# Loading x and wk in alternating halves, computing the first segment's K by token halves in four chunks, and casting its Q on ScalarE

## The chip, the cores and the metric

The kernel runs on 1 core of one Trainium2 chip. The metric is the device time of one execution in microseconds (us). Engines are called by the names of the profile: PE is TensorE's matrix multiply and PEld its weight load, DVE is VectorE, ACT is ScalarE, POOL is GpSimd, and SP is SyncE, which here only issues DMAs.

## What is computed

Two branches on the same 2048 x 512 input x (bf16) are mixed by a gate per token. Branch A is attention in four segments of 512 tokens, 32 heads of 16, with a memory carried from segment to segment; branch B is a gated GELU feed-forward with 1792 hidden units. Cut to what matters:

```python
q, k, v = x @ wq, x @ wk, x @ wv            # as (H=32, N=4 segments, L=512, Dh=16)
for s in range(N):
    logits = einsum('hqd,hkd->hqk', q[s], k[s]) * Dh**-0.5 + causal_mask
    a_dot = softmax(logits) @ v[s]
    a_mem = (phi(q[s]) @ M) / (phi(q[s]) @ z + 1e-6)
    outs.append(g * a_mem + (1 - g) * a_dot)
    M = M + phi(k[s]).T @ v[s];  z = z + sum(phi(k[s]))
a = concat(outs) @ wo
b = (gelu(x @ w_gate) * (x @ w_up)) @ w_down
out = sigmoid(x @ gate_w) * a + (1 - sigmoid(x @ gate_w)) * b
```

## The kernel before

**Layout.** Matmuls want the contracted dimension on the partitions, so x is held transposed: `xS[s]` is 128 x 4 x 512 (feature inside a block, 4 blocks `fc`, token). K, Q, gate and up projections of a segment are made in pieces of 128 output columns: four matmuls, one for each `fc`, of 128 x 128 weights against 128 x 512 tokens, summed in one bank of PSUM (2 KB a partition). A "chunk" c of K or Q is 128 columns, that is 8 heads; there are 4 chunks (`NC8`) a segment. Four banks are handed out in turn by the pool `pgen` (tag `gen`); the other four banks are one tile, `lg`, of the pool `plg`, which takes the logits of one visit.

**Start.** `load_inputs` (L136) issues all first loads on SP's queue in program order: x's first segment in two halves of 256 tokens into `x0` (L139, where a partition gets two neighbouring rows, so 2 KB in one run), then wk in two halves of 256 columns (L134, runs of 512 bytes), wq in one piece (runs of 1 KB), the gate weights, wv, beta and w_gate. PE first runs matmuls on constants (`warm_up`, L163). Then `transpose_x0` (L177) turns `x0` into `xS[0]`: for each half 8 transposes of 128 x 128 on PE into two banks, one bank copied out by DVE (L189) and one by ACT (L191); the copy also puts the tokens back in order, since a partition held two neighbouring ones. All 16 transposes come before any of K.

**K, Q, V and gate of segment 0.** `u_k` (L372) makes one chunk of K: 4 matmuls (L376), a cast to bf16 into `ktb` by `cast` (L306), and two masked copies of it into `KTm` (L386), a ring of `NK` = 3 chunks; the masks of the first three chunks run on DVE, the others on POOL. At the start chunks 0, 1, 2 of K are made, then the 4 chunks of Q (`u_q`, L286). `cast` puts an eviction on ACT when the planner's clock of ACT says that it is free within a limit, else on DVE; the limit is 0 until the main loop, so all casts of the start are DVE's (L313). Then `load_rest` (L151) issues the remaining loads: a memset on DVE of two elements of `xS[1]` (L152) holds back the transposing load of the second segment (L131), behind which w_up, the third segment, w_down and wo stand in SP's queue. V, a small piece `zT`, and the 14 gate pieces of segment 0 follow, the latter evicted by ACT with GELU.

**Main loop.** 72 visits, each of which makes a tile of logits (`group_qk`, L632: up to 8 matmuls into `lg`, one exponential on ACT, L643, causal masks on POOL, L647). Between visits a planner written in Python fills PE with pieces of other work from streams (K, Q, V, gate, up, down, out, memory), each with a due time (`want`) and a condition (`when`); it keeps its own clocks of PE, DVE and ACT, and the order of every engine's instructions is what it emits. K's fourth chunk of segment 0 is the first piece of stream K: it may start at visit 5 (`clock[0] >= last(i - NK)`), when the ring has room. Its 4 matmuls, its cast and its two masks on POOL lie in this filler; `phi` of chunks 2 and 3 of `ktb` stands behind it. A flag computed on the device chooses a general path that does not run with these inputs.

Of the kernel before, what the change touches and what calls it, by code (L numbers as in the profile page):

```python
# [11 lines left out]
ALU = mybir.AluOpType  # L12

P = 128
# [5 lines left out]
FC = D // P  # L20
NC8 = H // 8
# [3 lines left out]
NK = 3  # L25
NX = 3
NB = 8
# [4 lines left out]
BF = dt.bfloat16  # L32
F32 = dt.float32
# [3 lines left out]
MM512 = 0.216  # L37
# [16 lines left out]
def kernel(  # L54
# [15 lines left out]
    nc = tc.nc  # L70
# [4 lines left out]
    x2 = A_x[0]  # L75
# [5 lines left out]
    plg = ctx.enter_context(tc.tile_pool(name="plg", bufs=1, space=bass.MemoryType.PSUM))  # L81
    pgen = ctx.enter_context(tc.tile_pool(name="pgen", bufs=4, space=bass.MemoryType.PSUM))

    def const(shape, dtype, name):
        return cpool.tile(shape, dtype, name=name, tag=name)

    xS = [const([P, FC, L], BF, f"x{i}") for i in range(NX)]
    wq = const([P, FC, D], BF, "wq")
    wk = const([P, FC, D], BF, "wk")
# [5 lines left out]
    ident = const([P, P], BF, "ident")  # L95
    bm = const([P, 8, 17], BF, "bm")
    eo = const([P, 2], F32, "eo")
# [7 lines left out]
    ktb = const([P, NC8, L], BF, "ktb")  # L105
# [4 lines left out]
    KTm = const([P, NK, NB, 2, 64], BF, "KTm")  # L110
# [14 lines left out]
    def gen(name):  # L125
        return pgen.tile([P, 512], F32, name=name, tag="gen")
# [3 lines left out]
    def x_seg(s):  # L130
        nc.sync.dma_start_transpose(xS[s % NX][:, :, :], x2[s * L:(s + 1) * L, :])  # L131

    def cols(dst, src):
        nc.sync.dma_start(dst[:, :, :], src.rearrange("(fc p) n -> p fc n", p=P))  # L134

    def load_inputs():  # L136
        half = L // 2
        for i in range(2):
            nc.sync.dma_start(x0[:, 2 * i:2 * i + 2, :],  # L139
                              x2[half * i:half * (i + 1), :].rearrange("(p k) d -> p k d", p=P))  # L140
        for i in range(2):
            n = slice(D // 2 * i, D // 2 * (i + 1))
            cols(wk[:, :, n], A_wk[:, n])
        cols(wq, A_wq)
        nc.sync.dma_start(gw4, gate_w.rearrange("(fc p) -> fc p", p=P))
        cols(wv[:, :, 0:D], A_wv)
        nc.sync.dma_start(beta[:, :], A_beta.rearrange("(o n) -> o n", o=1).to_broadcast((P, H)))
        for n in (slice(0, 4 * P), slice(4 * P, DFF)):
            cols(wga[:, :, n], B_w_gate[:, n])

    def load_rest():  # L151
        nc.vector.memset(xS[1][:, 0, 0:2], 0.0)  # L152
        x_seg(1)
        cols(wup, B_w_up)
        x_seg(2)
        cols(wdn, B_w_down)
        cols(wo, A_wo)


    x0 = G[1][:, 0:KT, :]  # L160
    gw4 = G[1][0:FC, KT, 0:P]

    def warm_up():  # L163
        T = gen("warm")
        for i in range(5):
            nc.tensor.matmul(T[:, :], lhsT=nc.const_aps.tensor(1.0, [P, P], BF),
                             rhs=nc.const_aps.tensor(1.0, [P, 512], BF), start=True, stop=True)

        U = gen("warm")
        for i in range(16):  # L170
            j, r = i // 2 % 4, i % 2
            nc.tensor.matmul((T, U)[r][32 * j:32 * j + 32, 0:256],
                             lhsT=nc.const_aps.tensor(1.0, [64, 32], BF, 64 * r),
                             rhs=nc.const_aps.tensor(1.0, [64, 256], BF, 64 * r),
                             start=True, stop=True, tile_position=(64 * r, 32 * j))

    def transpose_x0():  # L177
        for half in range(2):
            for f0 in range(0, FC, 2):
                T = pgen.tile([P, 1024], BF, name="x0T", tag="gen")  # L180
                for i in range(4):
                    fc, k = f0 + i // 2, i % 2
                    nc.tensor.transpose(T[:, i * P:(i + 1) * P],
                                        x0[:, 2 * half + k, fc * P:(fc + 1) * P], ident[:, :])
                dst = xS[0][:, f0:f0 + 2, half * 256:half * 256 + 256].rearrange(
                    "q f (p k) -> q f k p", k=2)
                src = T[:, 0:512].rearrange("q (f k p) -> q f k p", f=2, k=2)
                if f0 == 0:
                    nc.vector.tensor_copy(dst, src)  # L189
                else:  # L190
                    nc.scalar.copy(dst, src)  # L191

    def transpose_gw():
        T = pgen.tile([P, 1024], BF, name="gwT", tag="gen")
        nc.tensor.transpose(T[:, 0:FC], gw4, ident[0:FC, 0:FC])
        nc.vector.tensor_copy(wv[:, :, D], T[:, 0:FC])
# [89 lines left out]
    def u_q(s, c):  # L286
        def f():
            T = gen("qT")
            for fc in range(FC):
                nc.tensor.matmul(T[:, :], lhsT=wq[:, fc, c * P:(c + 1) * P],  # L290
                                 rhs=xS[s % NX][:, fc, :],
                                 start=(fc == 0), stop=(fc == FC - 1))
                if fc < FC - 1:
                    yield MM512
            cast(QT[:, c, :], T[:, :])
            return MM512
        return 4 * MM512, EVAC, f


    limit = [0.0]  # L300
    spared = [0.0]

    def near(end):
        return t_act[0] - 1.0 <= end and max(t_act[0], end) + CAST_T <= limit[0]

    def cast(out, src, scale=1.0):  # L306
        end = t_pe[0] + MM512
        if near(end):
            nc.scalar.activation(out, src, AF.Copy, scale=scale)
            t_act[0] = max(t_act[0], end) + CAST_T  # L310
            spared[0] = EVAC
        elif isinstance(scale, float):
            nc.vector.tensor_copy(out, src)  # L313
        else:
            nc.vector.tensor_scalar_mul(out, src, scale)
# [7 lines left out]
    general_now = [False]  # L323
# [43 lines left out]
    def u_phk(s, c):  # L367
        def f():
            phi(ktb[:, c:c + 2, :], ktb[:, c:c + 2, :], ("k", s, c), 1)
        return 0.0, 0.0, f  # L370

    def u_k(s, c):  # L372
        def f():
            T = gen("kT")
            for fc in range(FC):
                nc.tensor.matmul(T[:, :], lhsT=wk[:, fc, c * P:(c + 1) * P],  # L376
                                 rhs=xS[s % NX][:, fc, :],
                                 start=(fc == 0), stop=(fc == FC - 1))
                if fc < FC - 1:
                    yield MM512  # L380
            cast(ktb[:, c, :], T[:, :])
            if general_now[0]:
                return MM512
            for p in range(2):
                eng = nc.vector if s == 0 and c < NK else nc.gpsimd
                eng.tensor_scalar(out=KTm[:, (NC8 * s + c) % NK, :, p, :],  # L386
                                  in0=ktb[:, c, :].rearrange("q (b k) -> q b k", b=NB),
                                  scalar1=eo[:, p:p + 1], scalar2=None, op0=ALU.mult)
            return MM512
        return 4 * MM512, EVAC, f  # L390

    def turn(dst, src):
        T = pgen.tile([P, 1024], BF, name="tT", tag="gen")
# [294 lines left out]
    load_inputs()  # L688
    make_identity(nc, ident[:, :])
    warm_up()  # L690
    transpose_x0()
    setup_consts()


# [7 lines left out]
    def unit(u, want, key=None, when=None):  # L702
        return u + (key, when, want)
# [78 lines left out]
    def run(u):  # L782
        if u[0] == 0.0:
            u[2]()
        else:
            for _ in u[2]():
                pass

    for c in range(NK):
        run(u_k(0, c))  # L790
    for c in range(NC8):
        run(u_q(0, c))
    load_rest()
    transpose_gw()
    for kt in range(KT):
# [25 lines left out]
    def first(i):  # L821
        return 9 * (i // 2) + (1 if i % 2 == 0 else 5)

    def last(i):
        return 9 * (i // 2) + (5 if i % 2 == 0 else 9)

    us = [unit(u_phk(0, 0), 0)]
    for i in range(NK, NSEG * NC8):
        s, c = i // NC8, i % NC8
        us.append(unit(u_k(s, c), first(i) - 12, ("k", s),  # L830
                       lambda i=i, s=s, c=c: clock[0] >= last(i - NK) and
                       (s == 0 or count(("pk", s - 1)) > c)))
        if c % 2 == 1 and s < NSEG - 1:
            us.append(unit(u_phk(s, c - 1), 0, None,
                           lambda s=s: s == 0 or count(("pk", s - 1)) == NC8))
    streams.append(Stream("K", us))
    us = []
    for i in range(NC8, NSEG * NC8):
        s, c = i // NC8, i % NC8
# [5 lines left out]
    us = []  # L845
# [7 lines left out]
    us = []  # L853
# [16 lines left out]
    us = []  # L870
    for s in range(NSEG - 1):
# [9 lines left out]
    us = [unit(u_absmax_x(2, (18, 20, 22, 25)), 17, None, lambda: clock[0] >= 17),  # L881
           unit(u_absmax_x(3, (52, 55, 56, 60)), 51, None, lambda: clock[0] >= 51),
           unit(u_bound(), 61, None, lambda: clock[0] >= 61)]
    streams.append(Stream("Z", us))

    us = []
# [6 lines left out]
    us = []  # L893
# [5 lines left out]
    us = []  # L899
# [6 lines left out]
    us = []  # L906
# [73 lines left out]
    for pieces in visits:  # L980
        clock[0] += 1
        for i, b, off in pieces:
            s, c = i // NC8, i % NC8
# [4 lines left out]
        s = pieces[0][0] // NC8  # L988
        t = group_qk(pieces)
# [8 lines left out]
        if lumps and lumps[0][0] == clock[0]:  # L998
            i = lumps.pop(0)[1]
# [156 lines left out]
    for reg in flag:  # L1156
        i = 0 if reg.engine == mybir.EngineType.Pool else 1
# [32 lines left out]
```

## Time and profile before

| what | value |
|---|---|
| time, median of 3 runs (lowest, highest) | 269.92 us (269.92, 272.15) |
| time of the profiled execution | 269.92 us |
| its span, first to last instruction | 268.2 us |
| granted TensorE clock, mean | 0.999 |
| K's matmuls in all (L376), 64 of 128x512 | 16.8 us |
| Q's matmuls in all (L290), 64 | 16.6 us |
| logit masks on POOL (L647), 256 | 113.9 us |
| exponentials on ACT (L643), 72 | 135.1 us |
| masks of K on POOL (L386), 26 | 40.6 us, 1571 ns each |
| DMA, share of 16 engines | 23.4% for the program's own queue, 16.14 MB |

Times inside the profile are in us from the start of the span. In a timeline a row is: start, duration, engine, line, operation, output<-inputs, shape, count; what stands in brackets is the idle time of that engine ahead of it and what ended it. In the chain of waits a row is start, duration and what the end of the program was waiting for in that stretch. Matmuls overlap: a 128x512 matmul has a record of 380 ns, but twelve of them follow each other in 2.6 us, 0.216 us each.

### The profile page before, as it was taken

The page shows a single profiled execution, that of the slowest core. Times are in us where ns is not written, and L with a number is a line of the kernel's source. Part 1 is how long each engine was busy: PE and PEld are TensorE (multiplying, and loading weights), DVE is VectorE, ACT ScalarE, POOL GpSimd, SP SyncE. Part 2 cuts the span into 40 slices and gives each one's busy share as a digit, 9 for nine tenths or more (in the row PEclk, how much of TensorE's full clock was granted, in tenths as well). Part 3 has the DMA queues.
Part 4 walks back from the last instruction along what each step waited for, and adds up shares of the span by engine and source line. Part 5 has one row for each costly group of instructions (what it writes and reads, how often), then busy time and mean ns, then how long its engine had stood idle before and what let it go on. Part 6 is the DMA issues. An engine that isn't in the chain of part 4 may idle for free.

```text
span 268.2 us, 6580 instructions
## 1 busy us (share of the span) xinstructions
PE 262.7 (98%) x2713; PEld 118.0 (44%) x2713; DVE 204.0 (76%) x391; ACT 209.0 (78%) x163; POOL 156.9 (58%) x298
## 2 busy tenths in 40 slices
PE   7999999999999999999999999999999999999994
PEld 3454434344454444544444444434454544344441
DVE  2999575968778787697985979686889479698364
ACT  3236889999997998889999988889888987657510
POOL 4000158897905979987921998596785079655500
PEclk9999999999999999999999999999999999999999
DMA  6999911200070000301032001100000200003102
GB/s 213 304 197 329 341 36 39 42 4 0 20 145 2 0 22 22 78 4 42 0 61 62 4 21 42 42 20 22 20 24 21 66 2 20 2 20 42 40 22 83
DMA packets 30281, 16.59 MB, mean 62 GB/s; under 512 B 20008, under 2 KB 28968, under 8 KB 30248
## 3 DMA queue, kind: packets, MB, share of 16 engines
q1 hardware_dynamic: 30248, 16.14, 23.4%
q8 instruction: 22, 0.36, 0.6%
q14 instruction: 11, 0.09, 0.1%
HBM read 8.14 MB, written 2.10 MB: 38 GB/s over the span
## 4 chain that ended last, share of the span: by engine, by line
PE 87%; POOL 5%; issue 4%; DMA 2%; ACT 1%; SPq 0%; DVE 0%; ACTq 0%; DVEq 0%; POOLq 0%
PE gT L473 19%; PE uT L494 17%; PE dT L510 14%; PE lg L638 8%; PE od L663 6%; PE aT L527 5%; PE qT L290 5%; PE kT L376 5%; PE vT L414 4%; POOL pT L647 3%; POOL KTm L386 2%; DMA wk<-in_A_wk_dram 2%; PE MT L548 1%; PE mn L617 1%; ACT pT L643 1%
## 5 line engine op out<-in xcount | busy, mean ns | idle before, releaser
L647 POOL TENSOR_SCALAR_AFFINE_SELECT pT<-pT 64x256 bf16<-64x256 bf16 x256 | 113.9, 445 | 94.3 <-ACT pT L643 81.5
L643 ACT ACTIVATE pT<-lg 128x2048 bf16<-128x2048 f32 x72 | 135.1, 1876 | 24.9 <-PE lg L638 21.6
L494 PE MATMUL uT<-x,wup 128*128 128x512 bf16 x224 | 60.4, 380 | 0.0
L473 PE MATMUL gT<-x,wga 128*128 128x512 bf16 x224 | 57.0, 380 | 0.0
L510 PE MATMUL dT<-wdn,G 128*128 128x512 bf16 x224 | 52.9, 380 | 0.0
L500 DVE TENSOR_TENSOR G<-uT,G 128x512 bf16<-128x512 f32 x56 | 38.1, 684 | 6.4 <-PE uT L494 6.2
L386 POOL TENSOR_SCALAR KTm<-ktb,eo 128x512 bf16<-128x512 bf16 x26 | 40.6, 1571 | 1.3
L670 DVE STREAM_TRANSPOSE oq<-od 128x512 f32<-128x512 f32 x32 | 21.0, 695 | 19.3 <-PE od L663 19.3
L510 PEld LDWEIGHTS <-G 128*128 128x128 bf16 x224 | 20.8, 98 | 25.0 <-issue 2.1
L473 PEld LDWEIGHTS <-wga 128*128 128x128 bf16 x224 | 20.4, 98 | 23.9 <-issue 2.2
L494 PEld LDWEIGHTS <-wup 128*128 128x128 bf16 x224 | 19.8, 97 | 24.0 <-issue 5.4
L638 PE MATMUL lg<-QT,KTm 32*128 32x192 bf16 (+7 forms) x512 | 28.6, 287 | 0.0
L313 DVE CAST G<-gT 128x512 bf16<-128x512 f32 x24 | 16.5, 688 | 9.7 <-PE gT L473 9.5
L638 PEld LDWEIGHTS <-KTm 32*128 32x128 bf16 x512 | 8.3, 92 | 28.3 <-issue 28.0
L663 PE MATMUL od<-pT,V 64*32 64x128 bf16 (+7 forms) x512 | 19.4, 284 | 0.2 <-POOL pT L647 0.2
L663 PE MATMUL od<-pT,Vs 64*32 64x128 bf16 (+7 forms) x512 | 19.4, 284 | 0.0
L488 ACT ACTIVATE G<-G 128x3584 bf16<-128x3584 bf16 x6 | 18.8, 3182 | 0.0
L676 DVE SCALAR_TENSOR_TENSOR o<-oq,ogs,rden 128x256 bf16<-128x256 f32 x32 | 17.0, 532 | 1.1
L376 PE MATMUL kT<-x,wk 128*128 128x512 bf16 x64 | 16.8, 380 | 0.7 <-DMA wk<-in_A_wk_dram 0.7
L290 PE MATMUL qT<-x,wq 128*128 128x512 bf16 x64 | 16.6, 379 | 0.0
L532 DVE SCALAR_TENSOR_TENSOR tB<-aT,gct,tB 128x512 bf16<-128x512 f32 x16 | 11.9, 746 | 6.0 <-PE aT L527 5.7
L527 PE MATMUL aT<-wo,oT 128*128 128x512 bf16 x64 | 16.5, 380 | 0.0
(96 smaller groups left out, 276.0 us busy)
## 6 DMA issues: line engine op xcount, KB each, us to landing
out_dram<-tB SPq DMA_DIRECT2D x16, 128.0 KB, 1.7
wup<-in_B_w_up_dram SPq DMA_DIRECT2D x1, 1792.0 KB, 8.7
wdn<-in_B_w_down_dram SPq DMA_DIRECT2D x1, 1792.0 KB
wga<-in_B_w_gate_dram SPq DMA_DIRECT2D x1, 1280.0 KB, 10.5
Vs<-V SPq DMA_DIRECT2D x8, 144.0 KB, 2.6
G<-in_A_x_dram SPq DMA_DIRECT2D x2, 256.0 KB, 2.8
wk<-in_A_wk_dram SPq DMA_DIRECT2D x2, 256.0 KB, 4.5
wq<-in_A_wq_dram SPq DMA_DIRECT2D x1, 512.0 KB, 5.8
```

What stands on the lines that cost most here:

```text
L290: nc.tensor.matmul(T[:, :], lhsT=wq[:, fc, c * P:(c + 1) * P], rhs=xS[s % NX][:, fc, :], start=(fc == 0), stop=(fc == FC - 1))
L376: nc.tensor.matmul(T[:, :], lhsT=wk[:, fc, c * P:(c + 1) * P], rhs=xS[s % NX][:, fc, :], start=(fc == 0), stop=(fc == FC - 1))
L386: eng.tensor_scalar(out=KTm[:, (NC8 * s + c) % NK, :, p, :], in0=ktb[:, c, :].rearrange("q (b k) -> q b k", b=NB), scalar1=eo[:, p:p + 1], ...
L473: nc.tensor.matmul(T[:, :], lhsT=wga[:, fc, hs * P:(hs + 1) * P], rhs=xS[s % NX][:, fc, :], start=(fc == 0), stop=(fc == FC - 1))
L494: nc.tensor.matmul(T[:, :], lhsT=wup[:, fc, hs * P:(hs + 1) * P], rhs=xS[s % NX][:, fc, :], start=(fc == 0), stop=(fc == FC - 1))
L500: nc.vector.tensor_tensor(out=g, in0=T[:, :], in1=g, op=ALU.mult)
L510: nc.tensor.matmul(T[:, :], lhsT=G[s % NG][:, hs, qt * P:(qt + 1) * P], rhs=wdn[:, hs, :], start=(hs == 0), stop=(hs == HS - 1))
L527: nc.tensor.matmul(T[:, :], lhsT=oT[:, fc, qt * P:(qt + 1) * P], rhs=wo[:, fc, :], start=(fc == 0), stop=(fc == FC - 1))
L638: nc.tensor.matmul(lg[:, j, off:off + n], lhsT=KTm[rows, i % NK, b].rearrange("r p k -> r (p k)"), rhs=QT[rows, i % NC8, 64 * b:L], start= ...
L643: nc.scalar.activation(pT[:, :, :], lg[:, :, :], AF.Exp, scale=DH ** -0.5)
L647: nc.gpsimd.affine_select(out=v, in_=v, pattern=[[0, 4], [1, 64]], compare_op=ALU.is_ge, fill=0.0, base=0, channel_multiplier=-1)
L663: nc.tensor.matmul(od[p][32 * j:32 * j + 32, 64 * b:L], lhsT=w[:, 18 * h:18 * h + 32], rhs=t[rows, j, off:off + n], start=(b == 0), stop=( ...
```

## The change

The loads go out as x half, wk half, x half, wk half; x's rows are taken so that partition p holds row 128 k + p (runs of 1 KB in place of 2 KB), and the copies after the transposes no longer reorder. A new function `first_k` makes all four chunks of segment 0's K, each in two halves of 256 tokens (8 matmuls of 256 columns a chunk): chunks 0 and 1 in banks of the ring, 2 and 3 in two banks of the logits' tile. Its order on PE is: transposes of half 0; chunks 0 and 1 of half 0; transposes of half 1; chunks 2 and 3 of half 0; chunks 0 and 1 of half 1; chunks 2 and 3 of half 1. DVE casts chunks 0 and 2, ACT 1 and 3. Q's four casts go to ACT by a flag. The planner's unit for the fourth chunk now holds only its two masks on POOL, and its due time and condition stay. `setup_consts` now comes ahead of the transposes in the program, so DVE's two small sums of `eo` stand ahead of its copies.

```diff
         for i in range(2):
             nc.sync.dma_start(x0[:, 2 * i:2 * i + 2, :],
-                              x2[half * i:half * (i + 1), :].rearrange("(p k) d -> p k d", p=P))
-        for i in range(2):
+                              x2[half * i:half * (i + 1), :].rearrange("(k p) d -> p k d", p=P))
             n = slice(D // 2 * i, D // 2 * (i + 1))
             cols(wk[:, :, n], A_wk[:, n])
...
-    def transpose_x0():
-        for half in range(2):
-            for f0 in range(0, FC, 2):
...
-                dst = xS[0][:, f0:f0 + 2, half * 256:half * 256 + 256].rearrange(
-                    "q f (p k) -> q f k p", k=2)
-                src = T[:, 0:512].rearrange("q (f k p) -> q f k p", f=2, k=2)
...
+    def transpose_x0(half):
+        for f0 in range(0, FC, 2):
...
+            dst = xS[0][:, f0:f0 + 2, half * 256:half * 256 + 256]
+            src = T[:, 0:512].rearrange("q (f t) -> q f t", f=2)
...
     def cast(out, src, scale=1.0):
         end = t_pe[0] + MM512
-        if near(end):
+        if on_act[0]:
+            nc.scalar.copy(out, src)
+        elif near(end):
...
+    def u_km(s, c):
+        def f():
+            k_masked(s, c)
+        return 0.0, 0.0, f
+
+    def first_k():
+        lg = plg.tile([P, 4, 512], F32, name="lg", tag="lg")
+        Ts = {2: lg[:, 0, :], 3: lg[:, 1, :]}
+
+        def part(c, half):
+            t = slice(256 * half, 256 * half + 256)
+            for fc in range(FC):
+                nc.tensor.matmul(Ts[c][:, t], lhsT=wk[:, fc, c * P:(c + 1) * P], rhs=xS[0][:, fc, t],
+                                 start=(fc == 0), stop=(fc == FC - 1))
+
+        def evict(c):
+            if c % 2 == 0:
+                nc.vector.tensor_copy(ktb[:, c, :], Ts[c][:, :])
+            else:
+                nc.scalar.copy(ktb[:, c, :], Ts[c][:, :])
+
+        transpose_x0(0)
+        for c in range(2):
+            Ts[c] = gen("kT")
+            part(c, 0)
+        transpose_x0(1)
+        part(2, 0)
+        part(3, 0)
+        for c in range(2):
+            part(c, 1)
+            evict(c)
+            k_masked(0, c)
+        part(2, 1)
+        part(3, 1)
+        evict(2)
+        k_masked(0, 2)
+        evict(3)
...
-    transpose_x0()
     setup_consts()
...
-    for c in range(NK):
-        run(u_k(0, c))
+    first_k()
     for c in range(NC8):
+        on_act[0] = True
         run(u_q(0, c))
+    on_act[0] = False
...
-        us.append(unit(u_k(s, c), first(i) - 12, ("k", s),
+        us.append(unit((u_km if i < NC8 else u_k)(s, c), first(i) - 12, ("k", s),
```

`k_masked` is the two masked copies, moved out of `u_k` unchanged.

More of the change, by code (lines that the diff above doesn't have):

```diff
@@ L175, in warm_up @@
                              start=True, stop=True, tile_position=(64 * r, 32 * j))
-    def transpose_x0():
-        for half in range(2):
-            for f0 in range(0, FC, 2):
[L180 to L184, printed above, removed]
-                dst = xS[0][:, f0:f0 + 2, half * 256:half * 256 + 256].rearrange(
-                    "q f (p k) -> q f k p", k=2)
-                src = T[:, 0:512].rearrange("q (f k p) -> q f k p", f=2, k=2)
[L188 to L191, printed above, removed]
+    def transpose_x0(half):
+        for f0 in range(0, FC, 2):
+            T = pgen.tile([P, 1024], BF, name="x0T", tag="gen")
+            for i in range(4):
+                fc, k = f0 + i // 2, i % 2
+                nc.tensor.transpose(T[:, i * P:(i + 1) * P],
+                                    x0[:, 2 * half + k, fc * P:(fc + 1) * P], ident[:, :])
+            dst = xS[0][:, f0:f0 + 2, half * 256:half * 256 + 256]
+            src = T[:, 0:512].rearrange("q (f t) -> q f t", f=2)
+            if f0 == 0:
+                nc.vector.tensor_copy(dst, src)
+            else:
+                nc.scalar.copy(dst, src)
     def transpose_gw():
@@ L300 @@
     limit = [0.0]
+    on_act = [False]
     spared = [0.0]
@@ L370, in u_phk, with k_masked @@
         return 0.0, 0.0, f
+    def k_masked(s, c):
+        for p in range(2):
+            eng = nc.vector if s == 0 and c < NK else nc.gpsimd
+            eng.tensor_scalar(out=KTm[:, (NC8 * s + c) % NK, :, p, :],
+                              in0=ktb[:, c, :].rearrange("q (b k) -> q b k", b=NB),
+                              scalar1=eo[:, p:p + 1], scalar2=None, op0=ALU.mult)
     def u_k(s, c):
@@ L375, in f @@
             for fc in range(FC):
-                nc.tensor.matmul(T[:, :], lhsT=wk[:, fc, c * P:(c + 1) * P],
-                                 rhs=xS[s % NX][:, fc, :],
+                nc.tensor.matmul(T[:, :], lhsT=wk[:, fc, c * P:(c + 1) * P], rhs=xS[s % NX][:, fc, :],
                                  start=(fc == 0), stop=(fc == FC - 1))
@@ L381, in f @@
             cast(ktb[:, c, :], T[:, :])
[L382 to L388, printed above, removed]
+            if not general_now[0]:
+                k_masked(s, c)
             return MM512
         return 4 * MM512, EVAC, f
+    def u_km(s, c):
+        def f():
+            k_masked(s, c)
+        return 0.0, 0.0, f
[10 more added lines that the diff above has]
+                nc.vector.tensor_copy(ktb[:, c, :], Ts[c][:, :])
+            else:
+                nc.scalar.copy(ktb[:, c, :], Ts[c][:, :])
[15 more added lines that the diff above has]
+        evict(3)
     def turn(dst, src):
```

## The prediction

> **What bounds the kernel now.** I read the page first: its spans, its busy times and its chain of work that ended last.
>
> ```profile
> span 268.2 us, 6580 instructions
> ...
> PE 262.7 (98%) x2713; PEld 118.0 (44%) x2713; DVE 204.0 (76%) x391; ACT 209.0 (78%) x163; POOL 156.9 (58%) x298
> ...
> PE 87%; POOL 5%; issue 4%; DMA 2%; ACT 1%; SPq 0%; DVE 0%; ACTq 0%; DVEq 0%; POOLq 0%
> ```
>
> PE is busy for all but 5.5 us. A record of a matmul is longer than its turn, so I checked with the waits of PE from 30 us to the end, which has one row (total, times, longest):
>
> ```profile
> PE od L663 <- POOL pT L647: 0.2, 1, 0.2
> ```
>
> So behind the start PE runs on without a gap that matters: work taken from PE there shortens the run by its own length, and a delay of the start lengthens it by its own. Everything hangs on the first 13 us. The chain of waits has them so:
>
> ```profile
> 1.71 4.35 DMA wk<-in_A_wk_dram
> 6.05 0.05 issue
> 6.10 2.76 PE kT L376 x12
> 8.87 3.45 PE qT L290 x16
> ```
>
> The start waits for the first half of wk, then is PE's. The timeline shows what stands around it:
>
> ```profile
> 0.97 2.31 PE L166 MATMUL warm<-const-bfloat16-1.0 128*128 128x512 bf16 x5 [0.97 <-PEq L1174]
> ...
> 3.77 1.59 PE L183 MATMUL x0T<-ident,G 128*128 128x128 bf16 x16
> ...
> 4.42 1.48 DVE L189 COPY x<-x0T 128x512 bf16<-128x512 bf16 x2 [4.42 <-PE x0T L183]
> 4.84 1.32 ACT L191 COPY x<-x0T 128x512 bf16<-128x512 bf16 x2 [2.71 <-PE x0T L183]
> ...
> 6.10 2.76 PE L376 MATMUL kT<-x,wk 128*128 128x512 bf16 x12 [0.74 <-DMA wk<-in_A_wk_dram]
> ...
> 8.58 3.25 PEld L290 LDWEIGHTS <-wq 128*128 128x128 bf16 x16 [0.21 <-DMA wq<-in_A_wq_dram]
> 8.70 3.62 PE L290 MATMUL qT<-x,wq 128*128 128x512 bf16 x16
> ...
> 10.94 2.48 DVE L313 CAST QT<-qT 128x512 bf16<-128x512 f32 x4
> ...
> 13.37 0.06 DVE L152 MEMSET x<- 128x1 uint32 x1
> ...
> 13.47 2.49 SPq L131 DMA_TRANSPOSE x<-in_A_x_dram  x1
> ```
>
> PE idles 0.74 us ahead of K, and Q starts at 8.70. Last, the landings, from the rows of x's load and of tile wk (first and last issue, then least, median and greatest time to landing):
>
> ```profile
> L139 SPq DMA_DIRECT2D G<-in_A_x_dram x2: 399/406/412, 0.8 to 1.2; - x2
> ...
> DMA to landing us min/median/max: 2.7/2.8/2.9
> ```
>
> ```profile
> L134 SPq DMA_DIRECT2D wk<-in_A_wk_dram x2: 427/467/507, 1.7 to 2.2; - x2
> ...
> DMA to landing us min/median/max: 4.3/4.5/4.7
> ```
>
> x's halves land at 0.8 + 2.7 = 3.5 and 1.2 + 2.9 = 4.1, wk's at 1.7 + 4.35 = 6.05 and 2.2 + 4.7 = 6.9, and wq at 2.7 + 5.8 = 8.5 (5.8 from the page's DMA issues). The gaps between landings are 0.65 (x, 256 KB in runs of 2 KB), 1.9 (first of wk), 0.85 (second, runs of 512 B), 1.6 (wq, 512 KB in runs of 1 KB).
>
> **Removed.** The fourth chunk's 4 matmuls leave the main loop: 4 x 0.216 (12 in 2.60 us, 6.10 to 8.70) = **-0.86 us** on PE, which is the path there. Its cast (0.69 on DVE or 0.6 on ACT) goes too; neither is the path.
>
> **Added at the start.** Before, K could run as soon as the first half of wk was there (chunk 2 needs the second only at 7.8). Now chunks 2 and 3 of half 0 stand on PE ahead of three quarters of the work that could otherwise go on, so the start waits for the second half of wk, the last of the four loads. The four loads have the same bytes in another order. With the gaps above, x 3.5, wk 5.4, x 6.05, wk 6.9. x's runs are now 1 KB: the nearest row in length is wq's, 1.6 / 2 = 0.8 for 256 KB against 0.65, so 0 to +0.15 a half; I take +0.15, as that row has this run length, and get wk at 5.55, x at 6.35, wk at 7.2.
>
> The Trainium skill ("DMA: Bandwidth & Descriptors", Specifications) holds 512 B enough for line rate, so 1 KB runs would cost nothing more and the net below would be 0.3 less; the gaps of 0.65, 0.8 and 0.85 for 256 KB speak against it.
>
> On PE, a matmul of 256 columns is half of 0.216, 0.108; its weight load takes 98 ns and runs beside the matmul ahead of it. Transposes of half 0 from 3.77 (8 weight loads there took 0.77) to 4.6; DVE's copy 4.42 to 5.16 (1.48 / 2), ACT's 4.84 to 5.50 (1.32 / 2): ready when wk lands at 5.55. Chunks 0 and 1 of half 0: 8 x 0.108 to 6.46. Transposes of half 1, 8 at half of a 0.108, 0.45: to 6.9; their copies end by 7.65 on both engines. From 7.25 the 24 other matmuls, 24 x 0.108 = 2.6: first chunks 2 and 3, which cover the copies until 8.1 (later copies would cost their lateness), so K ends at 9.85. wq is there by 8.5 + 0.3 = 8.8. **Q starts at 9.85, 1.15 later than 8.70.**
>
> **Moved, at no cost, with its cover.** Q's casts on ACT: 0.66 each (a copy of L191's kind) against 0.86 of PE per chunk. ACT then has the exponential for beta (0.23) and a table load (1.28) and is done near 15.7; the first gate result, before at 16.94, comes at 18.1. Without that cover of 2.4 us ACT would hold the gate's banks. DVE loses 2.48 of casts; it must cast chunk 0, mask it, and then mask chunk 1, for which it waits on ACT's cast; queued behind are chunk 2's cast and masks and the memset of L152. From chunk 0's end near 8.75 that is 2 casts of 0.69 and 6 masks of 0.31 (L386, 1.8 us for six): to 12.0, against 13.37. So SP's transposing load of x goes out about 1.4 earlier, and with it w_up, x, w_down, wo and V's copies behind it. The gate weights stand ahead of all of these; their second piece lands at 5.6 + 10.5 = 16.1 and is needed by the fifth gate piece at 15.9 + 4 x 0.86 + 1.15 = 20.5, so it has 4 us of cover. The masks of chunk 3 stay on POOL (2 x 1.57), and need not follow a matmul any more.
>
> **The planner's order.** With one piece less it emits another order on PE from visit 5 on, until late in the third segment; the fourth segment's is the same, word for word. The few waits of before in the part that changes are worth 0.3 at most; what the new order has can't be seen, so -0.3 to +1.5, and I take 0.
>
> **Sum:** 1.15 - 0.86 = +0.29 on a span of 268.2; outside it lie 269.92 - 268.2 = 1.72, and the profiled time is the median. So **270.2 us**.
>
> **Rivals.** *wk is early* (269.4). Its first half came 1.9 behind x, its second 0.85: if that excess of 1.05 hides once x follows wk, the last load lands near 6.15 and PE is the limit: from 5.3 (DVE's copy at 5.16, ACT's at 5.50) 32 x 0.108 + 0.45 = 3.9, Q at 9.2, net 0.5 - 0.86 = -0.35, and with a wait lost in the new order 269.4. For it: the excess is a single one. Against: both orders read a new tensor at that place.
>
> *The clock stays low* (271.7; the slower side). The profile grants a clock of 1.00 throughout, but the first matmuls are slow: the transposes' rows have both speeds.
>
> ```profile
> L183 PE MATMUL x0T<-ident,G x16: 219/314/314, 3.8 to 5.1; 128*128 128x128 bf16 x16
> ```
>
> Warm-up matmuls of 512 columns follow each other at 0.425 against 0.216 later, and the change to 219 ns falls near 4.8, after 3.8 us of unbroken work. In the new order PE falls silent at 4.6, before that point. If it must then work another 3.8 us from 5.55, to 9.35, it does only 1.9 us' worth of its 3.9, ends K at 11.35, and loses 1.5 against my 9.85 (271.7). It decides if the spell is broken by the silence from 4.6. The Trainium skill ("TensorE: Matmul & The Clock Gate", Part 1) tells of a free-running window of some 3.4 us that must be busy; by it the next chance is 4.8 + 3.4 = 8.2, K ends near 10.85 and the time is 271.2. By the trace only 0.2 us is missing from the spell, so I give it little.
>
> *The new order stalls* (271.3). One meeting of PE with POOL's masks in the fourth segment costs tenths of a us; a few of them, 1 us more. The like can be in the second and third segments now, as ACT is busy for 26.0 to 28.2 of each 30 us between 60 and 150.
>
> **How the numbers follow.** Forecast 0.52; early wk 0.17; low clock 0.12; stalls 0.15; the last 0.04 is for something larger. 1% is 2.7 us, about what a measurement tells from no change. PE's work bounds a gain to 0.35 + 0.3 and a few tenths, so faster by 1% gets 0.02. Slower by 1% needs a low clock and stalls together, or stalls of 2.4: 0.08. The rest, 0.90, is within 1%. The range takes in early wk at its lower end and the low clock at the upper one: 269.2 to 271.8.
>
> **What would show it.** Right: PE's wait ahead of the logits' banks (`lg`, by first_k) ends with DMA wk at 6.9 to 7.2; Q's first matmul near 9.85; the first logits 1.15 later than 28.06; 48 of K's matmuls left with 512 columns. Wrong: Q before 9.3 (early wk); matmuls of 256 columns 0.21 apart behind 5.5 (clock); copies of half 1 ending behind 8.1; PE waits in the second or third segment of more than 0.5 in sum.

## The result, and the profile after

The changed kernel took 271.61 us (median of 22 runs), the kernel before 270.01 in as many on the same chips: a ratio of 1.0051, with a 95% interval of 1.004 to 1.0062. That is 1.4 us slower (1.1 to 1.7): within the 1% that counts as no change, but well resolved. In a few executions of a kernel (2 of the 22 of before, 4 of the 12 of four_chunks_v11 below) the time is some 2 us above the rest; the medians are over all. The profiled execution took 271.57 us, 1.65 more than that of before. The forecast was 270.2, so its sign was right and its size was 1.4 short. The rival "The new order stalls" had said 271.3 and had a chance of 0.15.

The same lines of the page, after:

```profile
span 269.8 us, 6614 instructions
...
PE 263.0 (97%) x2729; PEld 119.2 (44%) x2729; DVE 200.4 (74%) x386; ACT 210.8 (78%) x168; POOL 156.6 (58%) x298
...
PE 84%; POOL 5%; issue 4%; ACT 2%; DMA 2%; SPq 1%; DVE 0%; ACTq 0%; DVEq 0%; POOLq 0%
```

The span is 1.6 longer than 268.2. PE has 16 matmuls more (halves in place of whole ones) and is busy for 0.3 more, so most of the 1.6 is time in which it stood still. ACT's share of the chain went from 1% to 2%, which is the first hint of where.

Next the waits of PE from 30 us to the end (total, times, longest):

```profile
PE uT L533 <- ACT V L309: 1.0, 2, 0.5
PE od L702 <- POOL pT L686: 0.2, 1, 0.2
```

The second row is the one that before had. The first is new: twice, the up projection of the MLP (`uT`) waits for ACT's cast of V. This view counts only time without any record of PE, and a record of a matmul lasts longer than its turn. Measured between the starts of the matmuls, each of the two costs 0.68, as is worked out below.

The chain of waits through the start, after (start, duration, what):

```profile
2.34 4.89 DMA wk<-in_A_wk_dram
7.23 0.05 issue
7.28 1.05 PE lg L405 x8
8.33 0.88 PE kT L405 x8
9.20 0.87 PE lg L405 x8
10.07 3.45 PE qT L287 x16
```

Before, the load in this place was wk's first half, landed at 6.05. Now it is the second, the last of the four loads, at 7.23. Three groups of eight matmuls follow, and then Q. The timeline of after shows the rest of the start, and the first logits:

```profile
3.77 0.66 PE L181 MATMUL x0T<-ident,G 128*128 128x128 bf16 x8
...
4.72 1.20 PE L405 MATMUL kT<-x,wk 128*128 128x256 bf16 x8 [0.29 <-DVE x L186]
...
6.32 0.62 PE L181 MATMUL x0T<-ident,G 128*128 128x128 bf16 x8 [0.41 <-DMA G<-in_A_x_dram]
6.75 0.42 DVE L186 COPY x<-x0T 128x512 bf16<-128x512 bf16 x1 [2.09 <-PE x0T L181]
6.98 0.58 ACT L188 COPY x<-x0T 128x512 bf16<-128x512 bf16 x1 [1.93 <-PE x0T L181]
...
7.28 1.05 PE L405 MATMUL lg<-x,wk 128*128 128x256 bf16 x8 [0.34 <-DMA wk<-in_A_wk_dram]
...
9.91 3.62 PE L287 MATMUL qT<-x,wq 128*128 128x512 bf16 x16
...
11.78 1.57 ACT L307 CAST QT<-qT 128x512 bf16<-128x512 f32 x3
11.87 0.06 DVE L151 MEMSET x<- 128x1 uint32 x1
11.95 4.14 SPq L131 DMA_TRANSPOSE x<-in_A_x_dram  x1
...
29.27 0.39 PE L677 MATMUL lg<-QT,KTm 32*128 32x512 bf16 x4
```

PE now waits three times ahead of Q: 0.29 for a copy, 0.41 for x's second half, 0.34 for wk's. Q starts at 9.91 instead of 8.70, 1.21 later, and the first logits are 1.21 later as well (29.27 against 28.06). The memset that lets SP load x again came 1.5 earlier than before.

Last, one of the two places in the main loop. PE's timeline of after around 129 us:

```profile
128.29 0.36 PE L453 MATMUL vT<-wv,x 128*128 128x448 bf16 x1
128.49 0.67 PE L587 MATMUL MT<-V,pk 128*128 128x136 bf16 x8
...
129.67 0.38 PE L533 MATMUL uT<-x,wup 128*128 128x512 bf16 x1 [0.51 <-ACT V L309]
```

and ACT's, for the same stretch:

```profile
127.31 1.88 ACT L682 ACTIVATE pT<-lg 128x2048 bf16<-128x2048 f32 x1 [0.25 <-PE lg L677]
129.08 0.54 ACT L309 ACTIVATE V<-vT 128x448 bf16<-128x448 f32 x1
130.49 1.88 ACT L682 ACTIVATE pT<-lg 128x2048 bf16<-128x2048 f32 x1 [0.87 <-PE lg L677]
```

V's last matmul is done near 128.65. Its bank has to be cast by ACT, but ACT has an exponential from 127.31 to 129.19 and casts only then, until 129.62. In the ring of four PSUM banks V's bank is followed by two banks of `od` and one of `MT`, so that the fifth piece, `uT`, wants V's bank back, and PE reaches it with only eight short matmuls in between. They end at 129.16; `uT` starts at 129.67. The record shows 0.51 idle. As a matmul's record is some 0.17 longer than its turn, PE lost 0.68. The same happens once more, where `uT` starts at 198.26. V has nine casts on ACT in this trace; for the other seven the view of waits shows none.

So the account of the span is: start +1.21, removed matmuls -0.86, the two waits +1.36 less 0.18 that before lost at one wait of this kind (behind DVE's cast of V, at 132.8). The sum is +1.53; the spans differ by 1.59, and 0.06 in small gaps has no name. What the start and the removed matmuls leave, 1.59 - 0.35 = 1.24, is the price of the new order.

### The profile page after: what moved, and what is told of

Same layout as the page of the kernel before. It is cut to its first block, busy times and chain, and to the rows that moved or that the text cites. A ratio compares the mean times of both kernels' runs of the same rounds, so it can differ in the third digit from the quotient of the medians.

```text
span 269.8 us, 6614 instructions
## 1 busy us (share of the span) xinstructions
PE 263.0 (97%) x2729; PEld 119.2 (44%) x2729; DVE 200.4 (74%) x386; ACT 210.8 (78%) x168; POOL 156.6 (58%) x298
## 4 chain that ended last, share of the span: by engine, by line
PE 84%; POOL 5%; issue 4%; ACT 2%; DMA 2%; SPq 1%; DVE 0%; ACTq 0%; DVEq 0%; POOLq 0%
PE gT L512 18%; PE uT L533 17%; PE dT L549 14%; PE lg L677 8%; PE od L702 5%; PE aT L566 5%; PE qT L287 5%; PE vT L453 4%; PE kT L383 3%; POOL pT L686 3%; POOL KTm L375 2%; ACT pT L682 2%; DMA wk<-in_A_wk_dram 2%; PE MT L587 1%; PE mn L656 1%
## 5 line engine op out<-in xcount | busy, mean ns | idle before, releaser
L313 DVE CAST G<-gT 128x512 bf16<-128x512 f32 x27 | 18.5, 684 | 5.9 <-PE gT L512 5.7
L702 PEld LDWEIGHTS <-V 64*32 64x32 bf16 x512 | 13.1, 92 | 5.9 <-issue 3.5
## 6 DMA issues: line engine op xcount, KB each, us to landing
wga<-in_B_w_gate_dram SPq DMA_DIRECT2D x1, 1280.0 KB, 10.5
```

What stands on the lines that cost most here:

```text
L702: nc.tensor.matmul(od[p][32 * j:32 * j + 32, 64 * b:L], lhsT=w[:, 18 * h:18 * h + 32], rhs=t[rows, j, off:off + n], start=(b == 0), stop=( ...
```

## The experiments

Each experiment was timed beside the kernel before, in the same rounds, and the ratio is to that; it is not the quotient of the medians.

| run | median, us | ratio (95%) |
|---|---|---|
| changed kernel | 271.61 | 1.0051 (1.0040, 1.0062) |
| e1_old_order | 270.88 | 1.0035 (1.0024, 1.0047) |
| e2_old_start | 271.26 | 1.0045 (1.0031, 1.0059) |
| e3_v_on_dve | 271.56 | 1.0055 (1.0039, 1.0071) |
| e4_runs_2k | 272.20 | 1.0092 (1.0067, 1.0116) |
| m8_both_gone | 270.26 | 1.0010 (1.0001, 1.0019) |
| m105_one_gone | 269.86 | 0.9993 (0.9985, 1.0002) |
| m12_both_gone | 270.58 | 1.0016 (1.0007, 1.0025) |
| best_old_loads | 270.03 | 1.0003 (0.9994, 1.0012) |
| q_on_dve | 271.64 | 1.0070 (1.0057, 1.0082) |
| before_m105 | 269.77 | 0.9998 (0.9989, 1.0007) |
| four_chunks_m9 | 270.45 | 1.0027 (1.0012, 1.0042) |
| four_chunks_v11 | 270.39 | 1.0029 (1.0005, 1.0054) |

Two theories stood against each other at first. **P**: the start costs 0.35 net (1.21 less the removed 0.86), and the rest, about 1.25, is the two waits that the planner's new order makes. **S**: the later start costs its whole 1.2, nothing of the 0.86 is given back, and the waits are only a sign of slack spent elsewhere. A third, **O**, came later: any rearranged order loses about as much.

**Order and start apart.** In e2_old_start the loads and the start are those of before, but with all four chunks of K there, so that the planner has one piece less; PE's order in the main loop is then that of the changed kernel. Against before, cut to what matters:

```diff
-    for c in range(NK):
+    for c in range(NC8):
         run(u_k(0, c))
...
-        us.append(unit(u_k(s, c), first(i) - 12, ("k", s),
+        us.append(unit((u_km if i < NC8 else u_k)(s, c), first(i) - 12, ("k", s),
```

> The kernel before with all four chunks of K made at its start in the old form (x, x, wk, wk; whole 512-column matmuls; Q cast by DVE), and the fourth chunk's matmuls gone from the loop: the main-loop order of PE is that of the changed kernel. Theory P: Q starts at 8.70 + 0.86 = 9.56, gives 0.86 back, and the new order's waits of 1.25 stay: 271.1 to 271.4, with both waits at the V casts in the trace. Rival S: the later start of 0.86 alone, 270.7 to 271.0, waits or not.

It took 271.26. Q started at 9.50, 0.80 later than before. Its waits of PE:

```profile
PE uT L501 <- ACT V L309: 1.0, 2, 0.5
```

These are the same two waits with none of the change's loads, halves or casts. The sum by P is 0.80 - 0.86 + 1.24 = +1.18; the spans differ by 1.18, the medians by 1.26. Behind the start PE loads the same weights in the same order in both kernels, and this one is ahead of the changed one by 0.41 us at Q and by 0.42 at the end: what the start costs goes through to the end, and the rest is the order's. S gave 271.0 at most, and falls.

The opposite kernel, e1_old_order, keeps the whole changed start and brings back the old order: the unit that now only masks still books four matmuls and a cast in the planner, without issuing them.

```diff
     def u_km(s, c):
         def f():
+            for fc in range(FC - 1):
+                yield MM512
+            end = t_pe[0] + MM512
+            if near(end):
+                t_act[0] = max(t_act[0], end) + CAST_T
+                spared[0] = EVAC
             k_masked(s, c)
-        return 0.0, 0.0, f
+            return MM512
+        return 4 * MM512, EVAC, f
```

> The changed kernel, but the planner still books the fourth chunk of K (864 ns of PE and a cast) without emitting its matmuls or cast, so the main loop has the order of before on every engine, less those instructions. Theory P (the loss is 0.35 net at the start and 1.25 of waits that the new main-loop order brings): the two waits of 0.68 at the V casts are gone, 270.2 to 270.5. Rival S (the later start costs its 1.2 in full, because the visits are paced by ACT and give nothing back for the matmuls taken out): 271.2 to 271.6, order or not.

270.88 lies between the two expectations. The two waits for V are gone, as P said, but a new one stands in the waits of PE:

```profile
PE lg L684 <- ACT pT L689: 0.6, 1, 0.6
```

```profile
43.55 0.40 PE L684 MATMUL lg<-QT,KTm 32*128 32x512 bf16 x4 [0.58 <-ACT pT L689]
```

(the second from PE's timeline). The matmul ahead starts at 42.59 and takes 0.216, so 0.74 is lost. The hole that the four matmuls left, booked but empty, was not filled: PE came to the logits' bank early by most of the 0.86 and waited for the exponential that reads it. So this kernel mixes both questions and decides neither. What it teaches is that work taken out of PE was a gain here only where something else was put in its place.

**Where the wait goes if V's cast is moved.** In e3_v_on_dve the two casts go to DVE, with the planner's books as they were, so that PE's order stays.

```diff
-    def cast(out, src, scale=1.0):
+    def cast(out, src, scale=1.0, dve=False):
...
-            nc.scalar.activation(out, src, AF.Copy, scale=scale)
+            if dve:
+                nc.vector.tensor_copy(out, src)
+            else:
+                nc.scalar.activation(out, src, AF.Copy, scale=scale)
...
-                 T[:, 0:DV].rearrange("q (h p d) -> q h p d", h=HV // 2, p=2))
+                 T[:, 0:DV].rearrange("q (h p d) -> q h p d", h=HV // 2, p=2),
+                 dve=(s, kt) in ((2, 2), (3, 2)))
```

> The changed kernel with two of V's casts (segments 2 and 3, third piece) emitted on DVE in place of ACT, the planner's books unchanged, so PE's order is the same. Theory P, with the waits caused by ACT, which does the cast only behind an exponential while PE needs that bank: both waits of 0.68 go, 270.2 to 270.6. If they only move to the next bank or to the exponential: 271.4 to 271.6. Rival S: 271.6, no change.

271.56: nothing came back. The two waits shrank to 0.25 each, but DVE, with 0.6 more to do, was now late with the product of gate and up projection, and `uT` waited for that bank instead, 0.84 between starts:

```profile
PE uT L537 <- DVE G L543: 0.7, 1, 0.7
```

So ACT's cast was what the two waits waited for, but the time alone does not part the theories here: S, too, had expected 271.6.

**Other orders.** The remaining test of P and O is to give the planner another due time for one kind of unit (`M`, the state's update), which shifts the order in which banks follow each other, and nothing else:

```diff
-        us += [unit(u_M(s, half), NP * s + 10 + 2 * half, ("M", s),
+        us += [unit(u_M(s, half), NP * s + 8 + 2 * half, ("M", s),
```

with 8, 10.5 or 12 for the 10.

> The changed kernel with one constant of the planner altered: the due time of the two memory pieces MT is 8 in place of 10. By PE's order, the two places where a bank of the ring is wanted again 0.5 us of PE work after V's last matmul are gone, and no new place under 0.7 us comes in. Theory P (those two waits are 1.2 to 1.3 of the loss): 270.1 to 270.6. Rival O (any order loses about as much; the waits turn up elsewhere, as they did when the casts went to DVE): 271.3 to 271.9.

> The same with 10.5 in place of 10: by PE's order the second of the two places (fourth segment's V) is gone, the first stays. Theory P: half of it back, 270.8 to 271.1, with one wait of 0.68 at a V cast near 129. Rival O: 271.3 to 271.9.

> The same with 12: both places gone, by another order. Theory P: 270.1 to 270.6. Rival O: 271.3 to 271.9.

With 8 both waits are gone, Q starts at 9.91 as in the changed kernel, and the time is 270.26: 0.25 above before (0.03 to 0.51), where P's 1.21 - 0.86 gives 0.35; by S it would have been 271.2. Of waits for another engine, PE's view from 30 us on has only the row that before has, too:

```profile
PE od L702 <- POOL pT L686: 0.2, 1, 0.2
```

With 12 both are gone as well, and one of another kind is there (`od` for DVE's product; the 64 matmuls of `od` in that visit took 1.07 longer):

```profile
PE od L702 <- DVE G L539: 0.7, 1, 0.7
```

Its 270.58 lies in P's bounds by luck: the wait for POOL near 230 us is absent there, which about makes up for the new one, and its profiled run (270.88) had Q only at 10.30. With 10.5 one of the waits for V is left, and yet the time is the least of all, 269.86, a whole us below what P expected. What P left out is again the wait for POOL, which is absent here as well. The view of waits gives it as 0.2, but PE loses more there, as the matmuls of `od` run several at a time and their records hide the gaps. The first matmul of that visit's 64 and one of the last, in the changed kernel and in m105_one_gone:

```profile
229.74 0.39 PE L702 MATMUL od<-pT,V 64*32 64x512 bf16 x1
...
231.69 0.19 PE L702 MATMUL od<-pT,Vs 64*32 64x64 bf16 x1
```

```profile
229.11 0.39 PE L702 MATMUL od<-pT,V 64*32 64x512 bf16 x1
...
230.08 0.19 PE L702 MATMUL od<-pT,Vs 64*32 64x64 bf16 x1
```

1.95 against 0.97: the wait costs 0.98, in before as in the changed kernel. With it the two profiled executions agree: Q at 10.17 (+0.26), one wait at V less (-0.68), no wait for POOL (-0.98), in sum -1.40, and the spans differ by 1.39. O, by which all of these lose alike, fell with 8 and 10.5.

**The start by its parts.** In e4_runs_2k x is loaded in runs of 2 KB again, and its copies sort the columns as before; everything else is the changed kernel.

```diff
-                              x2[half * i:half * (i + 1), :].rearrange("(k p) d -> p k d", p=P))
+                              x2[half * i:half * (i + 1), :].rearrange("(p k) d -> p k d", p=P))
...
-            dst = xS[0][:, f0:f0 + 2, half * 256:half * 256 + 256]
+            dst = xS[0][:, f0:f0 + 2, half * 256:half * 256 + 256].rearrange(
+                "q f (p k) -> q f k p", k=2)
-            src = T[:, 0:512].rearrange("q (f t) -> q f t", f=2)
+            src = T[:, 0:512].rearrange("q (f k p) -> q f k p", f=2, k=2)
```

> The changed kernel with x loaded in runs of 2 KB as before (and the copies reordering tokens again). If the run length costs 0.15 a half, as the prediction took: the second half of wk lands near 6.9 in place of 7.23, Q starts near 9.6 in place of 9.91, 271.2 to 271.4. If run length is nothing: landing at 7.2, 271.6; if the slower reordering copies matter, 271.6 to 271.9.

wk's second half landed at 7.14, against 7.23 with runs of 1 KB in the changed kernel and 7.09 in e1_old_order, so the run length bought nothing that can be told from chance, and the kernel was 0.6 slower than the changed one. Its timeline shows where:

```profile
7.10 0.73 DVE L187 COPY x<-x0T 128x512 bf16<-128x512 bf16 x1 [1.96 <-PE x0T L181]
7.19 0.28 PE L406 MATMUL lg<-x,wk 128*128 128x256 bf16 x1
7.32 0.73 ACT L189 COPY x<-x0T 128x512 bf16<-128x512 bf16 x1 [1.75 <-PE x0T L181]
7.88 0.93 PE L406 MATMUL lg<-x,wk 128*128 128x256 bf16 x7 [0.41 <-DVE x L187]
...
10.39 1.46 PE L288 MATMUL qT<-x,wq 128*128 128x512 bf16 x5
```

The sorting copies take 0.73 on either engine, where the plain ones of the changed kernel took 0.42 and 0.58. PE starts one matmul on wk, then stands for 0.41 until DVE's copy ends, and Q starts at 10.39, 0.48 later. But the matmuls at which it stands are those of chunks 2 and 3 over the first half of the tokens, which this copy of the second half does not write. In e1_old_order, with plain copies, the same eight run on while both copies are still at work:

```profile
7.06 0.42 DVE L186 COPY x<-x0T 128x512 bf16<-128x512 bf16 x1 [2.22 <-PE x0T L181]
...
7.14 1.05 PE L412 MATMUL lg<-x,wk 128*128 128x256 bf16 x8
7.28 0.59 ACT L188 COPY x<-x0T 128x512 bf16<-128x512 bf16 x1 [1.86 <-PE x0T L181]
```

So with the sorting copies the program makes PE wait at the second matmul, where the first that reads the second half is the ninth. Why, no run shows; that the interleaved columns are taken for a region that overlaps the first half is a guess. The copies ended at 7.83 and 8.05, and by an estimate from the rows the ninth matmul would have come at 7.19 + 8 x 0.108 = 8.05: with the wait in its place the longer copies would have cost next to nothing.

In q_on_dve only Q's casts go back to DVE (`on_act` stays False).

```diff
     for c in range(NC8):
-        on_act[0] = True
         run(u_q(0, c))
```

> The changed kernel with Q's four casts back on DVE, nothing else; PE's order is unchanged. The prediction put this part at nothing: 271.4 to 271.8, Q and V of the start without waits. Rival: DVE, which still has chunk 2's cast and masks until 12, holds the banks that V's first pieces want, and the start is later by 0.2 to 0.7: 271.8 to 272.3.

271.64, with no difference from the changed kernel's 271.61 that is clear of noise: the intervals of the two ratios overlap. On DVE's timeline the memset that SP waits for is back at its old place behind the casts, with no effect on the time:

```profile
11.71 2.48 DVE L313 CAST QT<-qT 128x512 bf16<-128x512 f32 x4
...
14.14 0.06 DVE L151 MEMSET x<- 128x1 uint32 x1
```

In best_old_loads the loads come in the old order (x, x, wk, wk) with runs of 1 KB and plain copies, K's four chunks run whole, Q's casts are on DVE, and `M` is due at 8. Against before, cut to K and `M`:

```diff
-    for c in range(NK):
+    for c in range(NC8):
         run(u_k(0, c))
...
-        us += [unit(u_M(s, half), NP * s + 10 + 2 * half, ("M", s),
+        us += [unit(u_M(s, half), NP * s + 8 + 2 * half, ("M", s),
```

> Loads as before (x, x, wk, wk) but x in runs of 1 KB with the plain copies, four chunks of K at the start in whole 512-column matmuls, Q cast by DVE, due time 8 for the memory pieces. If the start is bound by the landing of wk's first half (6.05 in the profile before, 5.75 in the one of the old start) and the copies (0.42 in place of 0.74 on DVE) no longer hold K, Q starts at 9.3 to 9.55, so -0.25 to 0 net of the 0.86, with no V waits: 269.6 to 270.1. Rival O: 270.9 or more.

270.03, on the level of before. K started at 6.24 and Q at 9.70, 0.2 earlier than in the changed kernel and 1.00 later than before: with 0.86 saved that is +0.14, where +0.03 was measured. Beside m8_both_gone (270.26, the same due time and the same order of PE behind the changed start) it shows that loading in turns, halving K and moving Q's casts bring nothing over the old order of the loads.

**A version better than both?** Three kernels tried to get rid of the wait for POOL in the fourth segment: before_m105 is the kernel before with `M` due at 10.5; four_chunks_m9 and four_chunks_v11 are best_old_loads with `M` due at 9, and with `M` back at 10 and V due one visit later.

```diff
-        us += [unit(u_M(s, half), NP * s + 8 + 2 * half, ("M", s),
+        us += [unit(u_M(s, half), NP * s + 9 + 2 * half, ("M", s),
```

```diff
-        us += [unit(u_v(s, kt), NP * s - 12 + 2.7 * kt, ("v", s),
+        us += [unit(u_v(s, kt), NP * s - 11 + 2.7 * kt, ("v", s),
```

> The kernel before with one constant of the planner altered, the due time of MT 10.5 in place of 10. In every trace so far PE's 0.73 of waits for POOL's masks near 230 came with one order of the down and out pieces about visit 66, and was absent in the two kernels without that order; this kernel is without it too. Theory P (the planner's order alone is worth a us either way): 269.1 to 269.6. Rival (the wait is bound to the fourth segment's pace, whatever the order): 269.9 to 270.2.

> Four chunks of K at the start with the loads x, x, wk, wk and plain copies, due time of MT 9: by PE's order neither the two places at V nor the one at visit 66. Start net 0 to 0.15 as in the run with due time 8, less the 0.73 at POOL's masks: 269.2 to 269.6. Rival (a gain in order is lost elsewhere): 269.9 to 270.3.

> The same start, MT's due time back at 10, V's due times one visit later (11 in place of 12): another order without any of the three places. Theory P: 269.2 to 269.6. Rival: 269.9 or more.

None did, and P missed all three, by 0.2, 0.9 and 0.8 us. The reading of PE's order ahead of the runs did not hold for the wait for POOL: it was in all three traces, with 0.76, 1.23 and 0.90 lost in that visit's `od` against 0.98 in before, and the last had 0.26 more at the tail. before_m105 comes to 269.77, a ratio of 0.9998, which is before. No kernel here is faster than before by more than its interval.

## Why the prediction was short by 1.4 us

- **Removed, -0.86**: the four matmuls are gone, and m8_both_gone shows the gain to be real where the planner refills the place. In e1_old_order 0.74 of it is lost again, where the place stays empty.
- **Added at the start, Q at 9.85**: 9.91 was measured, and wk's second half landed at 7.23 where 7.2 was forecast. The step holds, but two things in its working do not. The first half of wk came 0.83 behind x (4.54, not 5.55) and x's second half 1.73 behind that (6.27, forecast 6.35); the long gap moved from wk to the load after it. And the +0.15 for each half of x was not the price of runs of 1 KB. e4_runs_2k has 2 KB runs in the same order, and its landing lies among those with 1 KB. So 7.2 was met in part by luck: the 0.3 put down to the run length stands where x in fact came 0.2 later (3.71, not 3.5) and the gaps together 0.1 longer. The four loads in turns brought wk's second half at 7.1 to 7.6 in eight profiles, those in the old order at 6.8 to 7.3 in six, 0.2 sooner in the median, so the turns gain nothing at that landing. The rule of the Trainium skill that the prediction set against its rows ("DMA: Bandwidth & Descriptors", Specifications: 512 B are enough) was the better guide here: 7.14 with 2 KB, 7.23 with 1 KB.
- **The copies' cover**: forecast to end by 7.65, covered until 8.1. They ended at 7.17 and 7.56, as plain copies are shorter than the sorting ones (0.42 against 0.74 on DVE). e1_old_order shows the cover at work: ACT's copy ended at 7.87 there, and PE did not stop. In e4_runs_2k the copies ended ahead of 8.1 too (7.83 and 8.05), and PE stood all the same, as the program has it wait earlier. The sum had taken plain copies to last as long as the sorting ones of before, and ACT's at 0.66, half of its row; the two records of that row overlap, and each is 0.73.
- **Moved, at no cost**: right. q_on_dve undoes it, and nothing changes that is clear of noise; the memset came at 11.87 (forecast 12.0).
- **The planner's order, "-0.3 to +1.5, and I take 0"**: this is the term that was mis-sized. It measured +1.24, close to the upper bound. That the prediction took 0 had no reason from a row: it said that what the new order has can't be seen. e2_old_start shows it without the rest of the change, and m8_both_gone the rest of the change without it (270.26, where the forecast was 270.2). The prediction's own sign against itself, waits of PE of more than 0.5 in the second and third segment, came true with 1.0 in the same view. The rival "The new order stalls" was the nearer one, 0.3 short. The rival's place was right (second and third segment, ACT busy for nearly all of the time), but the mechanism named only a lack of time on ACT. What decided is which bank follows which: a cast that stands behind a 1.88 us exponential is harmless if PE has that long before it wants the bank, and here it had 0.5. The model of that rival, the meeting with POOL in the fourth segment, was read from the view of waits as tenths of a us, where it costs 0.98. PE's new order follows from the kernel alone and could be read ahead of any run; each `uT` that comes so few matmuls behind a V whose cast is ACT's could have been priced at up to an exponential.
- **wk is early**: fell. The excess of its first load did not hide; it went to the next load.
- **The clock stays low**: fell, and with a twist shown by e1_old_order, below. It set the upper end of the range, so that 271.61 lies within it partly by luck: what set the end did not happen. The +1.5 of the planner's order, which did bound what happened, would have given 271.7.

One thing is not settled: why PE's wait for POOL near 230 us, the same in before, is absent in m105_one_gone and m12_both_gone alone. In the chain of waits of the changed kernel POOL's masks stand there one behind the other from 227 to 231.5 us; in that of m105_one_gone it is PE's own work.

## What to carry to other kernels

Where a list scheduler fills the engine that sets the time, taking a piece out can reorder much of what stands behind it (here everything from visit 5 until late in the third segment); go through the new order for each reuse of a PSUM bank and ask which engine must empty it, what long instruction stands ahead of that, and how many matmuls PE has in between. A known loss of this kind is worth more than the edit: here 1.24 us against a net 0.35. The view of idle time understated what PE lost, as records of matmuls overlap (0.2 for 0.98): measure between starts. And a load that PE needs whole was not made earlier here by splitting it into turns with another: its first half came 1.5 us sooner, its last 0.3 later.

## What was not expected of the hardware

The time at which matmuls change to their full rate differs between executions of nearly the same start. The rows of the transposes (least, median, greatest ns) of the changed kernel and of e1_old_order, which have the same instructions up to there:

```profile
L181 PE MATMUL x0T<-ident,G x16: 219/219/266, 3.8 to 6.7; 128*128 128x128 bf16 x16
```

```profile
L181 PE MATMUL x0T<-ident,G x16: 219/254/314, 3.8 to 7.0; 128*128 128x128 bf16 x16
```

In the first the change came near 3.9 us, in the second near 6.6, and PE's timeline of e1_old_order has the first eight half matmuls of K at the low rate, 1.91 us instead of 1.20:

```profile
4.89 1.91 PE L412 MATMUL kT<-x,wk 128*128 128x256 bf16 x8
6.63 0.61 PE L181 MATMUL x0T<-ident,G 128*128 128x128 bf16 x8
7.14 1.05 PE L412 MATMUL lg<-x,wk 128*128 128x256 bf16 x8
```

It cost nothing, as wk's second half came at 7.09 anyway, and Q started at 9.77. The change came some 1.7 us after the silence ahead of 4.89, not the 3.8 that the rival of the low clock had put there. The granted clock reads 1.00 for both. The Trainium skill ("TensorE: Matmul & The Clock Gate", Part 1) says that the window runs freely and that the change varies with its phase, by 0.5 us either way; the runs agree on the variation and show a wider one, 3.9 to 6.6 us. In the changed kernel the silences of 0.41 and 0.34 us behind the change did not bring the low rate back.

A copy of 128 x 512 bf16 from PSUM took DVE 0.42 us with columns in order and 0.73 with columns interleaved by two; ACT 0.58 and 0.73. The Trainium skill ("Advanced Engine Details and Errata", VectorE Performance Modes) asks for unit stride in the mode with two elements a cycle, which agrees with DVE's ratio of 1.7.
